# A gated recurrence with a gated feed-forward layer on one core: smaller feed-forward groups, split prefix sums, transposes by DMA, one pool of PSUM banks and a new order

## The chip, the cores and the metric

The kernel runs on one core of a Trainium2 chip. The time is the device time of one execution in microseconds (us); a kernel's figure is the median of its runs. Beside the times there is one profiled execution, whose span (first to last instruction) the views below are cut from. A core has five engines with a queue of instructions each, worked off in order: TensorE (PE, matrix products into PSUM), VectorE (DVE), ScalarE (ACT), GpSimd (POOL) and SyncE (SP, which issues most DMAs). PSUM has eight banks of 512 f32 columns in each of 128 partitions.

## The reference

Two stages. The first is a linear recurrence over 768 steps for 4 x 8 heads with a state of 48 x 48:

```python
mag = np.sqrt(a_re * a_re + a_im * a_im)
scale = np.minimum(mag, 0.999) / (mag + 1e-06)
a_re_n, a_im_n = (a_re * scale, a_im * scale)
for t in range(S):
    new_re = ar * S_re - ai * S_im
    new_im = ar * S_im + ai * S_re
    kv = np.einsum('bhd,bhe->bhde', k[:, :, t], v[:, :, t])
    S_re, S_im = (new_re + kv, new_im)
    y[:, :, t] = np.einsum('bhd,bhde->bhe', q[:, :, t], S_re)
```

The second takes y as 3072 tokens of 384 numbers: `gate = 1 / (1 + exp(-(x @ w_gate)))`, `val = x @ w_val`, result `(gate * val) @ w_out`, with 1536 inner columns (12 blocks of 128). Inputs and output are f32.

## The kernel before, in words

**Tiling.** The sequence is cut into 6 chunks of 128 steps. A slab is one chunk of one batch element, all 8 heads: 128 partitions (steps) x 384 columns (8 heads x 48). There are 24 slabs, chunk by chunk, in seven groups (`SIZES`: five of four slabs, two of two). The recurrence becomes, inside a chunk, a masked product of scores, and between chunks a state of 128 x 384 per batch element that is decayed and added to.

**Steps of a slab**, by the names that the order uses:

- `lr`, `la`: loads of a_re, a_im (L559, 192 KB each, in rows of 48 numbers). `sq`, `add`, `min` (L566 to L589): squares, sum, cap; `lna`, `lnm` logarithms; `inv` = exp(-ln a_re); `r` = a_im x inv; `atan` the angle (L687).
- `cl` (L618): the running sum of log magnitudes along the chunk, as an f32 product with a constant triangle `wl_t`; `ee` its exponentials; `scr`, `rbe`, `arr`: the last row goes through DRAM to become the decay of the state.
- `lk`, `lq`, `lv`: loads of k, q, v; `v16` casts v; `qke` multiplies q and k with `ee`.
- `ct` (L701 or L723): the running sum of the angle, in turns, as an f32 product with `wt_t`; `r16`, `nid` subtract the whole turns; `cr` keeps the last row for the next chunk, which `hop` adds into the next chunk's first row, one DMA for each slab (L714), or, in chunk 1, a product with `sel_t`. `ab`, `cs` (L766): absolute value, sine, cosine into an SBUF tile `cs`.
- `ks`, `qs` (L782): k and q times cosine and sine, as f16, 128 x 8 x 128. `tp` (L820): 16 transposes on PE and copies `qkT` (L827) for slabs 0 to 12; for slabs 13 to 23 (`CROSS`) two transposing DMAs on SP (`xk`, `xq`, L803).
- `sc` (L839), `mst` (L847): scores and mask; `kv`, `u`, `x16`, `P`: the state; `y` (L905, L907) and `y16`, its copy to f16; `xp`, `xt` (L925, L931): three transposes on PE and a copy give y with columns along partitions.

**Steps of a group's feed-forward part (MoE)**: for each of the 12 blocks `pg` and `pv` (L944), three products each over all slabs of the group at once (512 columns for four slabs, 256 for two); `tanh` on ACT (L954), `p` = (tanh + 1) x val on DVE (L960). For each slab `po` (L980), 12 products of 384 columns, `ot` (its eviction) and `st` (the store on SP). The weights come in nine casting DMAs on POOL's queue (`wg`, `wv`, `wo`).

**PSUM.** Two pools of four banks: `gen` for the recurrence, `moe` for the feed-forward part. One tile takes one bank.

**What sets the order.** Each step has a due time in the table `TIMES`. `Plan.order` sorts all steps by it, and the instructions go to their engines' queues in that sequence, so each queue, SP's and POOL's among them, is a fixed list. `SLOTS` says which buffer of its kind each tile takes. Where an engine changes its set of functions, a table load is put in (L1008). `WARM` puts filler products on `zero` ahead of some steps (L1014), 150 in all. `eng`, `scaled`, `SQV`, `ABV` and `ULATE` choose the engine of some elementwise steps.

Of the kernel before, what the change touches and what calls it, by code (L numbers as in the profile page):

```python
# [26 lines left out]
CROSS = 13  # L27
EASE = 0
ULATE = 4
BRISK = 1  # L30
PAIR = 2
PECARRY = 1
SQV = range(4, 9)
ABV = range(2, 9)
# [3 lines left out]
        22.939, 53.604, 46.761],  # L38
    "wv": [
        41.489, 57.377, 49.918],  # L40
    "wo": [
        69.384, 65.792, 74.71],
    "lr": [
        0.6, 2.76, 4.68, 1.01, 7.56, 11.4, 21.96, 9.48, 29.035, 36.763,
        34.603, 40.603, 53.574, 65.05, 65.46, 69.488, 91.541, 102.449, 94.661,
        101.489, 129.641, 144.257, 166.92, 169.283],
    "la": [
        1.42, 5.64, 6.6, 3.72, 8.52, 13.32, 21, 14.28, 30.955, 37.723, 44.224,
        38.683, 56.839, 59.355, 66.25, 71.918, 91.951, 100.699, 93.701,
        100.289, 132.576, 136.865, 169.693, 171.783],  # L50
    "sq": [
        5.29, 9.13, 10.09, 7.21, 12.09, 16.953, 26.869, 17.819, 35.119,
        43.141, 51.317, 50.58, 63.932, 71.041, 72.995, 77.727, 96.326, 108.9,
        100.923, 107.686, 141.821, 149.617, 173.785, 176.745],
    "add": [
        6.159, 9.999, 11.044, 8.079, 13.107, 17.97, 27.886, 19.639, 42.886,
        44.046, 52.222, 58.417, 64.837, 72.97, 75.53, 81.618, 99.728, 109.941,
        101.828, 108.978, 146.191, 151.929, 174.69, 177.65],
    "min": [
        10.579, 11.624, 21.17, 29.665, 54.424, 59.948, 80.715, 83.639,  # L60
        111.798, 110.895, 156.229, 185.814],
    "lna": [
        10.958, 34.211, 53.348, 80.235, 115.074, 157.704, 179.252],
    "lnm": [
        12.335, 32.834, 62.547, 84.606, 112.957, 159.31, 186.78],
    "inv": [
        13.712, 36.423, 64.669, 81.743, 117.191, 158.572, 180.12],
    "r": [
        16.087, 15.221, 39.728, 37.968, 67.623, 70.424, 89.8, 94.764, 118.736,
        126.526, 159.477, 181.025],  # L70
    "cl": [
        13.863, 16.67, 20.01, 15.378, 36.319, 37.411, 34.836, 38.883, 64.65,
        68.978, 65.942, 65.296, 86.871, 112.147, 102.388, 106.72, 115.007,
        117.823, 134.023, 131.882, 160.664, 162.183, 192.729, 188.19],
    "ee": [
        15.356, 20.801, 21.541, 20.061, 37.8, 38.54, 35.683, 39.73, 66.046,
        69.825, 68.557, 72.255, 87.718, 114.334, 111.477, 112.217, 116.451,
        118.669, 137.956, 136.74, 161.511, 163.03, 193.576, 189.037],
    "scr": [
        23.34, 22.65, 23.62, 22.37, 44.634, 48.008, 43.366, 48.288, 94.111,  # L80
        85.572, 83.333, 75.858, 96.031, 114.89, 112.033, 112.773, 118.11,
        120.772, 143.977, 139.687, 185.698, 186.798, 194.287, 194.567],
    "rbe": [
        31.915, 61.755, 97.571, 116.08, 149.099, 193.468, 197.428],
    "lk": [
        19.08, 12.36, 23.9, 10.44, 30.542, 22.93, 46.624, 26.99, 86.538,
        74.318, 80.523, 75.448, 103.409, 82.923, 106.289, 108.241, 133.536,
        118.468, 143.567, 127.135, 153.417, 186.388, 158.185, 173.993],
    "lq": [
        20.04, 18.12, 27.942, 16.2, 39.643, 35.803, 47.598, 49.079, 89.103,  # L90
        79.105, 83.883, 76.705, 104.369, 95.621, 107.249, 112.313, 135.905,
        125.596, 148.689, 134.624, 157.07, 193.058, 158.595, 187.724],
    "lv": [
        15.24, 17.16, 35.013, 42.956, 54.152, 67.21, 41.563, 81.87, 92.361,
        85.162, 115.54, 96.581, 105.329, 118.878, 87.987, 130.695, 139.277,
        121.052, 148.279, 126.005, 185.978, 192.648, 170.823, 177.453],
    "v16": [
        20.593, 42.309, 50.738, 49.342, 66.832, 77.757, 59.371, 87.463,
        98.286, 94.188, 124.976, 103.369, 118.084, 149.97, 105.026, 147.632,
        171.078, 133.794, 189.145, 130.048, 191.369, 202.109, 188.569, 183.572],  # L100
    "qke": [
        23.805, 22.502, 32.19, 20.947, 45, 47.581, 55.616, 60.85, 96.525,
        88.039, 91.561, 85.702, 112.701, 115.256, 128.287, 134.657, 148.209,
        164.194, 152.883, 143.564, 162.433, 196.377, 194.498, 198.138],
    "atan": [
        17.39, 41.764, 76.35, 105.833, 131.576, 183.842, 183.105],
    "ct": [
        18.918, 20.953, 26.326, 21.761, 43.292, 45.031, 52.079, 49.241,
        90.692, 86.225, 90.046, 89.232, 122.944, 118.469, 127.422, 128.468,
        141.143, 143.731, 163.053, 166.071, 196.201, 198.47, 197.014, 210.201],  # L110
    "r16": [
        19.765, 22.036, 28.601, 24.671, 44.785, 46.524, 55.711, 53.381,
        92.893, 87.268, 96.023, 92.427, 124.789, 119.316, 128.465, 129.397,
        145.892, 151.604, 163.899, 167.878, 197.481, 201.212, 205.333, 211.683],
    "nid": [
        21.599, 22.636, 29.201, 25.271, 47.8, 47.124, 57.969, 53.981, 95.223,
        89.07, 97.975, 98.138, 125.513, 120.184, 129.686, 131.483, 151.699,
        153.161, 165.483, 170.802, 198.308, 205.144, 206.601, 216.88],
    "cr": [
        25.889, 26.259, 30.065, 26.629, 49.053, 49.423, 59.91, 56.806, 95.586,  # L120
        95.956, 102.136, 104.169, 125.876, 126.246, 130.049, 132.953, 152.062,
        156.041, 176.375, 174.522],
    "cs": [
        23.575, 24.732, 30.542, 29.067, 49.793, 48.055, 58.646, 56.019,
        97.088, 89.752, 102.535, 99.273, 126.617, 120.704, 130.419, 133.335,
        153.726, 154.883, 165.847, 171.166, 198.671, 205.507, 207.141, 217.243],
    "ks": [
        25.137, 27.735, 34.253, 31.008, 53.847, 50.186, 62.767, 63.633,
        100.35, 91.041, 105.9, 103.014, 130.62, 121.993, 133.214, 138.058,
        155.016, 167.012, 173.321, 172.455, 201.678, 209.351, 208.486, 218.665],  # L130
    "qs": [
        26.003, 29.533, 35.985, 36.851, 56.177, 51.783, 69.053, 65.696,
        101.548, 97.554, 107.254, 108.12, 132.348, 123.325, 143.227, 141.296,
        157.143, 168.81, 175.386, 177.145, 203.143, 210.817, 215.684, 219.531],
    "ab": [
        30.542, 29.067, 49.12, 48.055, 58.364, 55.245, 97.088],
    "tp": [
        31.002, 27.003, 30.555, 36.965, 39.976, 38.436, 40.822, 42.338,
        64.204, 60.921, 63.757, 63.31, 71.142, 78.268, 80.861, 67.236,
        111.701, 114.56, 108.014, 104.329, 119.514, 113.24, 112.793, 121.647,  # L140
        155.897, 136.164],
    "qkT": [
        33.056, 33.654, 37.717, 38.315, 42.217, 39.084, 41.618, 43.881,
        65.097, 61.569, 67.856, 64.499, 73.684, 79.317, 83.445, 68.455,
        112.348, 115.942, 110.784, 109.586, 120.713, 114.145, 113.546,
        124.191, 156.545, 146.957],
    "sc": [
        39.752, 39.529, 41.273, 44.584, 47.577, 44.807, 46.784, 48.678,
        69.624, 75.674, 80.638, 79.114, 78.044, 81.308, 86.002, 84.728,
        117.176, 119.961, 115.653, 114.337, 127.199, 125.29, 117.599, 126.326,  # L150
        158.294, 153.974, 148.462, 148.686, 161.31, 159.167, 162.829, 160.041,
        177.84, 180.206, 182.371, 190.582, 191.856, 193.375, 188.836, 189.059,
        217.265, 217.042, 220.489, 220.712, 225.009, 222.435, 227.095, 226.217],
    "mst": [
        40.553, 39.953, 42.815, 45.85, 48.521, 45.251, 47.456, 49.586, 71.295,
        77.073, 81.062, 79.916, 78.711, 81.732, 86.669, 85.212, 117.6,
        121.312, 116.54, 115.343, 127.866, 126.187, 118.666, 126.786, 158.718,
        154.398, 148.887, 151.004, 161.781, 160.25, 163.254, 162.381, 179.769,
        180.968, 186.393, 191.006, 192.589, 193.799, 190.083, 189.483,
        218.066, 217.466, 220.913, 221.978, 227.064, 223.102, 227.663, 229.162],  # L160
    "kv": [
        40.622, 58.131, 77.844, 72.884, 102.188, 82.829, 122.094, 117.399,
        132.528, 134.669, 150.851, 145.025, 166.717, 170.965, 176.345,
        179.358, 201.706, 211.495, 207.411, 220.935],
    "P": [
        41.152, 60.655, 78.245, 74.282, 104.834, 84.746, 122.859, 118.2,
        142.162, 135.07, 153.269, 145.426, 169.676, 178.704, 183.373, 181.567,
        204.867, 213.384, 212.918, 221.512],
    "y": [
# [131 lines left out]
}  # L301
WARM = {
    ('cl', 0): 41,
    ('cl', 2): 8,
    ('cl', 3): 2,
    ('ct', 0): 7,
    ('ct', 2): 16,
# [737 lines left out]
```

## Time and profile before

| | us |
|---|---|
| median of 3 runs | 265.34 (264.82 to 265.72) |
| profiled execution, span | 263.2 |
| PE busy | 240.2 |
| DVE busy | 211.7 |
| ACT busy | 178.5 |
| POOL busy | 150.7 |
| DMA moved | 38.12 MB, mean 145 GB/s |

The page cuts the span into 40 equal slices of 6.6 us and gives each engine's busy share in tenths, the TensorE clock granted (PEclk) and the share of the 16 DMA engines. A group's line gives the source line, engine, operation, result and operands with shapes, the count, the busy sum and the mean time in ns of one, and then the engine's idle time ahead of it with what ended it. Products overlap in the pipeline, so their busy times are longer than the distance from one start to the next; the chain gives starts. The costliest groups by line:

| line | step | engine | count | mean ns |
|---|---|---|---|---|
| L944 | pg, pv of 512 columns | PE | 360 | 379 |
| L980 | po | PE | 276 | 326 |
| L960 | p of 512 | DVE | 60 | 682 |
| L954 | tanh of 512 | ACT | 60 | 606 |
| L847 | mst | DVE | 48 | 685 |
| L680 | qke | POOL | 20 | 1915 |
| L618 | cl, f32 | PE | 48 records | 557 |
| L931 | xt copy | DVE | 24 | 352 |
| L507 | y16 / ot | DVE | 24 / 23 | 551 |

### The profile page before, as it was taken

How to read it: one execution, taken by the hardware profiler on the slowest of the kernel's cores; microseconds unless marked ns; L12 is line 12 of the kernel's file. 1: busy time of each engine (PE TensorE's matmuls, PEld its weight loads, DVE VectorE, ACT ScalarE, POOL GpSimd, SP SyncE). 2: the span in 40 equal slices, each digit the busy share in tenths (PEclk: the TensorE clock that was granted, in tenths of full speed). 3: DMA queues.
4: the chain of work that ended last, by engine and by line, in shares of the span. 5: the costliest groups of instructions: out<-in, count | busy, mean ns of one | idle time of the engine just before them, and what ended most of it. 6: DMA issues, size and time to landing. Idle time of an engine off the chain costs nothing.

```text
span 263.2 us, 5644 instructions
## 1 busy us (share of the span) xinstructions
PE 240.2 (91%) x2066; PEld 150.2 (57%) x2066; DVE 211.7 (80%) x363; ACT 178.5 (68%) x288; POOL 150.7 (57%) x165
## 2 busy tenths in 40 slices
PE   6076598999999999999999999999999999999995
PEld 6043375454657654547765456654457544679784
DVE  2658998798988979979997889898859689987453
ACT  3799698299999478999469648758974373214240
POOL 3035409969599999679877299833687642010000
PEclk9669989999999999999999999999999999999999
DMA  7999999999999939975699969859964455651011
GB/s 146 218 214 176 192 149 188 205 166 182 139 205 202 181 74 169 176 157 95 121 209 204 151 135 149 194 111 178 221 133 90 66 110 108 73 147 36 8 54 60
DMA packets 174859, 38.12 MB, mean 145 GB/s; under 512 B 167768, under 2 KB 174832, under 8 KB 174832
## 3 DMA queue, kind: packets, MB, share of 16 engines
q1 hardware_dynamic: 170336, 34.20, 68.3%
q0 software_dynamic: 4496, 3.57, 9.7%
q8 instruction: 16, 0.26, 0.4%
q14 instruction: 11, 0.09, 0.1%
HBM read 30.74 MB, written 4.76 MB: 135 GB/s over the span
## 4 chain that ended last, share of the span: by engine, by line
PE 58%; ACT 15%; DMA 8%; DVE 7%; SPq 4%; issue 3%; POOL 3%; ACTq 0%; POOLq 0%
PE o L980 16%; PE v L944 13%; PE g L944 11%; PE cl L618 4%; ACT L1008 4%; DMA a<-in_a_im_dram 3%; PE sc L839 3%; SPq L541 3%; PE ct L723 3%; DMA a<-in_a_re_dram 3%; ACT a L687 2%; POOL qk L680 2%; DMA qk<-in_q_dram 2%; ACT g L954 1%; POOL a L609 1%
## 5 line engine op out<-in xcount | busy, mean ns | idle before, releaser
L954 ACT ACTIVATE g<-g 128x512 f16<-128x512 f32 (+1 forms) x84 | 43.6, 542 | 37.4 <-PE g L944 34.5
L960 DVE SCALAR_TENSOR_TENSOR p<-g,v 128x512 f16<-128x512 f16 (+1 forms) x84 | 49.6, 607 | 20.9 <-ACT g L954 10.1
L944 PE MATMUL v<-xt,wv 128*128 128x512 f16 (+1 forms) x252 | 57.3, 348 | 0.5 <-ACT g L954 0.4
L944 PE MATMUL g<-xt,wg 128*128 128x512 f16 (+1 forms) x252 | 56.9, 348 | 0.5 <-DVE xt L931 0.3
L980 PE MATMUL o<-wo,p 128*128 128x384 f16 (+1 forms) x300 | 54.6, 319 | 0.5 <-ACT g L954 0.5
L577 POOL TENSOR_TENSOR lm<-sq 128x384 f32<-128x384 f32 x20 | 23.2, 1174 | 30.7 <-DVE sq L568 18.9
L680 POOL TENSOR_TENSOR qk<-qk,ee 128x768 f32<-128x768 f32 x20 | 38.2, 1915 | 2.4 <-ACT ee L627 1.6
L847 DVE TENSOR_TENSOR mst<-sc,msk_t 128x512 f16<-128x512 f32 x48 | 32.3, 685 | 4.7 <-PE sc L839 4.6
L944 PEld LDWEIGHTS <-wv 128*128 128x128 f16 x252 | 24.1, 98 | 20.6 <-issue 1.6
L980 PEld LDWEIGHTS <-p 128*128 128x128 f16 x300 | 27.3, 97 | 14.9 <-issue 0.9
L944 PEld LDWEIGHTS <-wg 128*128 128x128 f16 x252 | 23.6, 97 | 20.3 <-issue 2.6
L618 PE MATMUL cl<-lm,wl_t 128*128 128x384 f32 x48 | 22.2, 557 | 9.2 <-ACT lm L598 8.9
L1008 ACT ACT_TABLE_LOAD x23 | 29.5, 1283 | 0.4
L782 DVE TENSOR_TENSOR qst<-qk,cs 128x768 f16<-128x768 f32 x24 | 26.1, 1092 | 0.0
L782 DVE TENSOR_TENSOR kst<-qk,cs 128x768 f16<-128x768 f32 x24 | 24.4, 1029 | 1.4 <-ACT cs L772 0.9
L609 POOL TENSOR_TENSOR a<-a 128x768 f32<-128x768 f32 x10 | 18.1, 1816 | 9.1 <-DMA qk<-in_q_dram 7.8
L571 ACT ACTIVATE sq<-a 128x768 f32<-128x768 f32 x19 | 16.0, 846 | 6.3 <-DMA a<-in_a_im_dram 6.2
L861 POOL TENSOR_TENSOR state<-state,arr 128x384 f32<-128x384 f32 x16 | 13.9, 869 | 11.0 <-DVE state L889 10.7
L827 DVE COPY qkT<-tp 128x1024 f16<-128x1024 f16 x26 | 17.3, 682 | 1.5 <-PE tp L821 1.5
L625 ACT ACTIVATE ee<-cl 128x384 f32<-128x384 f32 x24 | 12.0, 500 | 9.0 <-PE cl L618 6.9
L839 PEld LDWEIGHTS <-qkT 128*128 128x128 f16 x192 | 13.4, 97 | 7.4 <-issue 2.7
L723 PE MATMUL ct<-a,wt_t 128*128 128x384 f32 x40 | 16.9, 507 | 0.6 <-ACT a L687 0.5
(76 smaller groups left out, 428.9 us busy)
## 6 DMA issues: line engine op xcount, KB each, us to landing
a<-in_a_re_dram SPq DMA_DIRECT2D x24, 192.0 KB
a<-in_a_im_dram SPq DMA_DIRECT2D x24, 192.0 KB
qk<-in_k_dram SPq DMA_DIRECT2D x24, 192.0 KB
v<-in_v_dram SPq DMA_DIRECT2D x24, 192.0 KB
qk<-in_q_dram SPq DMA_DIRECT2D x24, 192.0 KB
out_dram<-ot SPq DMA_DIRECT2D x23, 192.0 KB
wg<-in_moe_w_gate_dram POOLq DMA_DIRECT2D x3, 384.0 KB, 6.4
wv<-in_moe_w_val_dram POOLq DMA_DIRECT2D x3, 384.0 KB, 6.4
```

Source lines behind the costliest of these rows:

```text
L577: eng(g).tensor_tensor(out=T[LM][:, s], in0=T[SQ][:, 0], in1=T[SQ][:, 1], op=ALU.add)
L618: nc.tensor.matmul(T[CL][:, :HD], wl_t, T[LM][:, s], start=True, stop=True)
L680: eng(g).tensor_tensor(out=T[QK], in0=T[QK], in1=T[EE], op=ALU.mult)
L723: nc.tensor.matmul(T[CT][:, :HD], wt_t, T[A][:, 1, s], start=True, stop=False, skip_group_check=True)
L782: nc.vector.tensor_tensor(out=T[SL][i].rearrange("p h (r x) -> p h r x", r=2)[:, :, :, 0:D], in0=heads(T[QK][:, i]).unsqueeze(2) .broadcas ...
L839: nc.tensor.matmul(sc[:, i], kt, qt, start=True, stop=True)
L847: nc.vector.tensor_tensor(out=T[MS], in0=T[SC], in1=msk_t.unsqueeze(1).broadcast_to([L, 4, L]), op=ALU.mult)
L944: nc.tensor.matmul(T[ACC][:, :nt], w[:, j, fb * 128:fb * 128 + 128], T[XT][:, j, :nt], start=(j == 0), stop=(j == 2))
L954: nc.scalar.activation(out=T[G16][:, :nt], in_=T[PG][:, :nt], func=FT.Tanh, scale=0.5)
L960: nc.vector.scalar_tensor_tensor(out=T[PT][:, fb, :nt], in0=T[G16][:, :nt], scalar=1.0, op0=ALU.add, in1=T[PV][:, :nt], op1=ALU.mult)
L980: nc.tensor.matmul(T[PO][:, :wd], T[PT][:, fb, s * L:(s + 1) * L], wo16[:, fb, c0:c0 + wd], start=(fb == 0), stop=(fb == NFB - 1))
L1008: nc.scalar.preload_act_table_set(SETS[key[1]])
```

## The change

Seven things at once:

- **MoE groups of two slabs.** `pg`, `pv`, `tanh`, `p` run over pairs of slabs (256 columns), two blocks of 128 inner columns in one bank, so that `tanh` and `p` still take 512 elements. 12 pairs x 6 double blocks.
- **Prefix sums as two f16 passes** for groups 2 to 6 (`SPLIT`, slabs 8 to 23): the operand is split into a high and a low f16 part (`lh`, `ll` for the logarithms, `th`, `tl` for the angles), and `cl` and `ct` are two f16 products each. The cap is taken after the logarithm there.
- **Cosine and sine in PSUM.** `ct`'s result lies in the second of two neighbouring banks, `ab` writes the first, both sines are taken in place, and `ks`, `qs` read them from PSUM.
- **y by transposing DMA** on SP (`xt`, slabs 4 to 23, `YCROSSED`), with no `xp` and no copy. q and k go by DMA from slab 9 on (`CROSSED`) instead of 13.
- **The hop by group.** The last rows of a chunk go to DRAM (`car`, on SP) and come back in one adding DMA per group.
- **One pool of eight PSUM banks** (`bank`), with views cut from one tile.
- **A new order**: new `TIMES`, `SLOTS` and `WARM` (26 fillers), and a table `HOME` that names the engine of each elementwise step; table loads go from 23 to 31.

Counts of instructions: DVE 48 `mst`, 72 `p`, 18 `qkT`, 14 `y16`, 12 `ot`, 8 `v16`, 7 `sq`, 10 `ab`, 8 `ll`, 8 `tl`; ACT 17 `sq`, 10 `y16`, 11 whole `ot` and 2 halves, 5 `v16`, 14 absolute values, 72 `tanh`; POOL 23 `qke`, 11 `v16`, 11 `x16`, 5 hops, 8 `r`, 7 `lh`, 5 `th`; SP 30 transposes of q and k and 20 of y. The core of the diff:

```diff
-CROSS = 13
+CROSSED = range(9, 24)
+YCROSSED = range(4, 24)
+SPLIT = range(2, 7)
+HOME = {
+    "sq": "aaavvvvaavaaaaaaavvaaaaa",
+    "y16": "aavvvavaavvvaaaavavvvvvv",
+    "ot": "vvavvvvaavvaaavvaavvaaaaa",
...
-    t_gen = kind("gen", 4, [L, 512], F32, psum)
-    t_moe = kind("moe", 4, [L, 512], F32, psum)
+    banks = psum.tile([L, 8, 512], F32, name="banks")
...
+            def e2(T, LM=LM, LH=LH, i=i, j=j, w=w):
+                home("lh", w).tensor_scalar(
+                    out=T[LH][:, 0, i:j], in0=T[LM][:, i:j], scalar1=LNCAP,
+                    scalar2=1.0, op0=ALU.min, op1=ALU.mult)
...
+                nc.vector.scalar_tensor_tensor(
+                    out=T[LH][:, 1, i:j], in0=T[LM][:, i:j], scalar=LNCAP,
+                    op0=ALU.min, in1=T[LH][:, 0, i:j], op1=ALU.subtract)
...
-                nc.tensor.matmul(T[CL][:, :HD], wl_t, T[LM][:, s],
-                                 start=True, stop=True)
+                for i in range(2):
+                    nc.tensor.matmul(T[CL][:, :HD], wl16, T[LH][:, i, s],
+                                     start=not i, stop=bool(i))
...
+                    nc.tensor.matmul(
+                        T[CS][:, 1, :HD], wt16 if split else wt_t,
+                        turns(T)[:, s, i] if split else T[A][:, 1, s],
+                        start=not i, stop=False, skip_group_check=True)
...
-                nc.scalar.activation(out=cs[:, 1], in_=ct, func=FT.Sin,
-                                     scale=TWO_PI)
+                nc.scalar.activation(out=T[CS][:, 1, :HD], in_=T[CS][:, 1, :HD],
+                                     func=FT.Sin, scale=TWO_PI)
...
-                    nc.gpsimd.dma_start(
-                        T[A][:1, 1, s], T[CRP][32 * b + 31:32 * b + 32],
-                        accum_op=ALU.add)
+                    nc.sync.dma_start(car[c - 1], T[CRP][31::32])
+                nc.gpsimd.dma_start(
+                    T[A][:1, 1, :n], car[c - 1][lo:lo + n].unsqueeze(0),
+                    accum_op=ALU.add)
...
+            if m in YCROSSED:
+                def e(T, Y16=Y16, XT=XT, s=s):
+                    nc.sync.dma_start_transpose(out=T[XT][:, s % PAIR],
+                                                in_=T[Y16])
...
-                    for j in range(3):
-                        nc.tensor.matmul(
-                            T[ACC][:, :nt], w[:, j, fb * 128:fb * 128 + 128],
-                            T[XT][:, j, :nt], start=(j == 0), stop=(j == 2))
+                        for r in range(2):
+                            f0 = (2 * fp + r) * 128
+                            for j in range(3):
+                                nc.tensor.matmul(
+                                    T[ACC][:, r], wt[:, j, f0:f0 + 128],
+                                    T[XT][:, :, j], start=(j == 0),
+                                    stop=(j == 2))
```

## The prediction

> **What bounds the kernel now.** I read four views: the page's slices, the busy times by stretch, the chain that ended last with its single pieces, and the groups by shape.
>
> ```profile
> PE 240.2 (91%) x2066; PEld 150.2 (57%) x2066; DVE 211.7 (80%) x363; ACT 178.5 (68%) x288; POOL 150.7 (57%) x165
> PE   6076598999999999999999999999999999999995
> PEclk9669989999999999999999999999999999999999
> DMA  7999999999999939975699969859964455651011
> ```
>
> The span has two parts. A ramp, in which PE has little to do while DMA is at 9 tenths, and a long stretch in which PE is full. The first real gate product stands at 58.65 us in the chain. The stretches (span, then PE, weight load, DVE, ACT, POOL, clock, DMA share, GB/s):
>
> ```profile
> 0.00:58.60 58.60, 40.58 (x345) 26.94 (x346) 44.12 (x81) 43.35 (x60) 27.89 (x37) 0.88 1.02 184
> 58.60:87.00 28.40, 28.35 (x239) 16.85 (x239) 25.12 (x37) 28.00 (x40) 24.53 (x29) 1.00 1.13 183
> 87.00:115.00 28.00, 26.99 (x199) 14.82 (x198) 25.41 (x39) 21.89 (x37) 23.85 (x23) 1.00 0.85 160
> 191.00:235.00 44.00, 43.97 (x371) 26.06 (x371) 35.88 (x63) 18.99 (x35) 19.93 (x24) 1.00 0.55 105
> ```
>
> From 58.6 to the last product at 260 PE is busy 199.6 of 201.3 us. The worst long stretch (87 to 115) has 96.4%. So the kernel is ramp 58.65 + PE work 201.3 + a tail of 3.3 (last eviction and store) = 263.2. DVE is second, at 88% even while PE is full. What PE's work costs there is read from consecutive starts in the chain, since busy records overlap:
>
> ```profile
> 205.28 0.17 PE xp L925 x3
> 206.15 0.65 PE g L944 x3
> 206.80 0.16 PE ct L737
> 206.96 0.65 PE ct L723 x2
> 233.51 0.22 PE sc L839 x4
> 235.27 0.33 PE v L944 x3
> ```
>
> An f32 product of 384 columns (L723, recorded as x2) takes 0.65, an f16 one of the same width (L737) 0.16. Three gate products 512 wide take 0.65, three 256 wide 0.33: the same per column.
>
> **The change, part by part. PE.** (1) Prefix sums of slabs 8 to 23 as two f16 passes: 16 cl and 16 ct go from 0.65 to 2 x 0.16, 32 x 0.33 = 10.6 us less. Both prices are rows of this trace, so the bounds are close (cl also shows 0.70: 11.4). (2) y by DMA for slabs 4 to 23: 60 PE transposes at 0.17/3 = 0.057, 3.4 less. (3) q and k by DMA from slab 9 on instead of 13: 64 transposes, 3.6 less. (4) MoE groups of two slabs: 864 products 256 wide against 360 of 512 and 144 of 256; by the rows above the time is the same (94 us), and tanh (L954) and gate product (L960) keep their 512-element shape with two blocks per bank. Sum: 17.6 us of PE. In the full stretch each of them is on the path, since nothing but PE bounds there.
>
> **The ramp.** The first gate product needs slabs 0 and 1 instead of 0 to 3. By the due times of the two orders, 36 input loads of 192 KB and 4 weight loads of 384 KB (as landed) stand ahead of it, against 47 and 5. That is 8.65 MB against 11.2; at the 184 GB/s of the first stretch, 47 us. The other gate is DVE: 75 instructions instead of 83 are queued ahead of its first gate product; at starts 0.47 apart for 384 elements, 0.6 for 512 and 1024, 0.87 for 768, that is 39 us instead of 45, and at today's density (45 in 60) 52 us for the first p, 50.5 for the product before it. I take 49; the bounds are 45 (58.65 scaled by bytes) and 55 (as now, less only the wait from the first pair's transposed y to the second's, 55.1 to 58.6, the DVE copies at 54.78 and 57.98). Ahead of the product PE then does 18.2 us of real work instead of 21.1 (3 sel/ct statements and a nid fewer, partly against kv), so 2.9 us move behind it. The order issues 26 filler products instead of 150, 6 of them ahead of the MoE. The clock in slices 2 and 3 is 0.6, and there a cl took 1.66 instead of 0.65. If it fell back so, the chain's own PE pieces of one slab (cl 0.65, ct 0.65, nid 0.16, transposes 0.46, scores 0.22, y 0.2) would double: 0 to +2.3, inside the bounds.
>
> [...]
>
> **Other engines** (today's means). DVE gains 16 low parts (ll, tl) of 768 elements at 0.95 as L568 = +15.2, 8 v16 at 0.3 to 0.56, say 0.4 = +3.2, two sq and two r at 0.95 = +3.8, three ab +1.7, lh/th +1.7, u and x16 +0.9; it loses 21 xt at 0.352 = 7.4, 10 y16 at 0.55 = 5.5, 11 whole and 2 half ot = 6.8, 8 qkT at 0.68 = 5.4, 3 qke = 3.2, and 1.9 in p. Net -3.7: 208 us. ACT gains 8 table loads:
>
> ```profile
> L1008 ACT ACT_TABLE_LOAD x23 | 29.5, 1283 | 0.4
> L782 DVE TENSOR_TENSOR qst<-qk,cs 128x768 f16<-128x768 f32 x24 | 26.1, 1092 | 0.0
> L803 SPq DMA_TRANSPOSE qkT<-qst x11: 1231/1286/2125, 130.5 to 229.4; - x11
> SPq L803 <- DVE p L960: 11.7, 4, 4.9
> ```
>
> that is +10.3, and 22 evictions at 0.49, two half ones, 9 copies at 0.52 and a th, less two sq and three abs: +24 in all, 202 us. POOL loses 15 (13 v16, 11 hops, 5 x16, 2 r, against 3 qke and 5 th). These ride under PE while they keep up. Behind the ramp, whose share I scale by the queued work (DVE 44.1 x 39/45 = 38, ACT 43.4 x 58/66 instructions = 38), DVE stands at (208-38)/187 = 91% and ACT at (202-38)/187 = 88%, against 83% and 67%. The stretch at 58.6 shows both that high (88% and 99%) with PE full, so it can be done, with less slack. I let PE fall from 99.2% to 97.5%, between today and the 96.4% of 87 to 115: 4.8 us given back; bounds 0 and 7 if today's rows carry over, up to 13 by the rival below.
>
> Cosine and sine in PSUM removes no instruction. Two of eight banks are held from ct to qs (some 6 us a slab, against one bank and about 4.5): about 24 x 7.5 = 180 bank-us more out of 1,500 (8 banks, 187 us). It is covered by the freer pool; without the cover PE waits, which is inside the give-back. The kst/qst group shows a mean of 1.03 and 1.09 with a median of 0.95: 24 x (0.08 + 0.14) = 5.2 us of stretching, single ones to 2.02 while POOL runs. I count 0, with 0 to 5.2 less as bounds. [...]
>
> SP: 28 transposes and 4 car stores more. At 1.28 each SP is held 36 us longer (an xt moves 3 blocks, not 8, so 0.5 to 1.28), and the 22 of before waited 35 us in all, 1.6 each. Queued behind each are the loads, with sq, qke and v16 waiting for them, and the scr and out stores. The transposed y is late by its issue and transfer, perhaps 3 us against 0.6 for transposes and copy; the gate products wait for it, covered by other groups' output products (0.65 a piece). The car store adds a trip ahead of hop (3.1 us to landing), under the MoE of the group before; uncovered, five times 3.
>
> **Sum.** 49 + (201.3 - 17.6 + 2.9 = 186.6, at 97.5% instead of 99.2%: +4.8 = 191.4) + 3.3 = 243.7, that is 19.5 below the profiled 263.2. The profiled execution stands 2.1 below the median of 265.34, so 246.
>
> **Rivals.** (a) PE is no longer the bound: DVE, with ACT beside it, sets the pace. For: 91% asked where the stretches from 87 to 235 show 86% (127 of 148). 170 us at 86% are 198 us: 49 + 198 + 3.3 = 250, plus 2.1 = 252; where the last 28 us can't be filled (55% now), 9 more: 252 to 261. The DMA rings give nearly the same: 38.1 + 4.1 MB (8 transposes of 262 KB, 20 of 98) with 1.2 in the last 28 us is 41 MB at 184 GB/s = 223 + 28 = 251; against it, slices of 259 GB/s. (b) Slower: the SP queue, in order, makes the loads late. Its issues now sum to 205 us of the 231 in which it is used, stretched to 2 to 5 us a piece wherever the rings are full (at the least durations, 0.37 for a load and 1.23 for a transpose, they would be 89). 28 x (1.28 + 1.6) = 81 more; if only the free 26 takes it up, loads slip by 55 at the end; half of that reaching PE gives 246 + 27 = 273. It decides once 20 us of slip reach PE. For: up to 88 us SP is never free. Against: behind 117 us it has gaps of several us, 12 of the 15 q/k pairs and 12 of the 20 xt are due later than that, and the 35 us of waits of now cost PE nothing visible. (c) The change doesn't do what it says: no gain from f16 passes would give back 10.6 and make 257. The L737 row makes this unlikely.
>
> **Numbers.** The forecast 0.58, spanning 237 to 252; (a) with (c) 0.24; (b) 0.15; no change 0.03. The range 236 to 258 holds the first nearly whole and most of (a): 236 is the 45 us ramp with nothing given back and cl at its 0.70, 258 the 55 us ramp with about 11 given back. Runs of this kernel tell 0.3% (0.8 us) from no change: faster 0.82, same 0.03, slower 0.15.
>
> **What would show it.** The first gate product near 49 us, PE above 97% from there, cl and ct as two f16 passes in 0.32 in the chain, DVE near 208 and ACT near 202, SP's waits on transposes (35 now) under 60. The forecast is wrong if PE idles more than 10 us behind the ramp, or the ramp passes 55: then the reading of which engine holds PE, not the count of PE's work, has failed.

## The result, and the profile after

The changed kernel takes 317.52 us (median of 4 runs, 316.14 to 324.62) where the kernel before takes 265.08 us (median of 4, 264.54 to 265.72): a ratio of 1.1971, 95% interval 1.1932 to 1.2009. The run of 324.62 us had a lower granted clock, 0.894 against 0.908, and is not in the ratio. The forecast was 246. The profiled execution spans 314.4 us.

The page of the changed kernel, its busy times and the slices of TensorE and its clock:

```profile
PE 237.2 (75%) x2178; PEld 175.5 (56%) x2178; DVE 207.1 (66%) x334; ACT 200.6 (64%) x313; POOL 147.8 (47%) x140
...
PE   0094899995997937598968649779759699779396
...
PEclk9998799999599996979999959887969789979989
```

The first line was forecast well: DVE 207.1 (208 expected), ACT 200.6 (202). But the row of nines that PE had in the kernel before is gone, and the granted clock dips with it. The stretch from the first gate product to the end, for the kernel before and then for the changed one (span, PE, weight load, DVE, ACT, POOL, clock, DMA share, GB/s):

```profile
58.60:263.20 204.60, 199.60 (x1721) 123.30 (x1720) 167.62 (x283) 135.19 (x229) 122.78 (x129) 1.00 0.72 134
```

```profile
48.60:314.40 265.80, 210.34 (x1985) 158.31 (x1982) 170.37 (x263) 162.44 (x261) 122.23 (x108) 0.90 0.68 126
```

The first gate product starts at 48.6 us, where 49 was forecast. All that went wrong lies behind it: 265.8 us instead of 194.7 (191.4 and the tail of 3.3). PE is busy 210.3 of them instead of 186.6, and idle 55.5 instead of 8.1. Those two, 23.7 and 47.4, less the 0.4 of the ramp, are the whole error of 70.7 in the span. The busy part is nearly all clock: the granted clock behind the ramp is 0.90, and with the same number of products, 2178, the kernel x11 below has PE busy for 214.1 us at 0.986 over the whole run, against 237.2 at 0.908 here.

Who waits for whom, over the whole span (engine, tile and line, what ended the wait: us, times, longest):

```profile
POOL qk L732 <- DMA qk<-in_q_dram: 23.8, 8, 5.6
...
PE banks L1054 <- DMA xt<-y: 19.8, 8, 4.8
...
PEld L922 <- DMA qkT<-kst: 12.2, 4, 5.7
...
ACT sq L592 <- DMA a<-in_a_im_dram: 10.7, 5, 3.4
```

Four kinds of transfers are late at once: the loads of q and k, the transposed y (`xt`), the transposed k, the loads of a. In the kernel before no DMA stands among the waits ahead of PE, whose largest are:

```profile
PE cl L618 <- ACT lm L598: 8.9, 2, 8.8
PE ct L737 <- DVE r L730: 3.8, 3, 1.9
```

What these four share is SyncE's queue, and these are its own waits at the y transposes (L1016):

```profile
SPq L1016 <- DVE y L523: 19.0, 3, 8.0
...
SPq L1016 <- DVE banks L839: 13.8, 2, 7.5
...
SPq L1016 <- DVE state L979: 10.5, 2, 7.0
```

All waits at L1016 add up to 69.9 us, those at the q and k transposes (L881) to 26.9: 96.8 for transposes, against 35 before. One such stand in the timeline of SyncE (start, duration, what is issued):

```profile
116.45 1.27 SPq L881 DMA_TRANSPOSE qkT<-kst  x1
117.77 0.57 SPq L561 DMA_DIRECT2D v<-in_v_dram  x1
126.11 1.19 SPq L1016 DMA_TRANSPOSE xt<-y  x1
127.34 0.57 SPq L561 DMA_DIRECT2D a<-in_a_re_dram  x1
127.96 0.53 SPq L747 DMA_DIRECT2D car<-cr  x1
128.54 0.45 SPq L561 DMA_DIRECT2D a<-in_a_im_dram  x1
129.09 2.01 SPq L881 DMA_TRANSPOSE qkT<-kst  x1
```

For 7.8 us, from 118.3 to 126.1, SyncE issues nothing, because y of one slab isn't ready (ScalarE's copy of it ends at 126.1). Then come, in one burst, the two loads, the carry and the k transpose that stood behind it. In the window from 110 to 130 us PE is busy 12.8 of 20 us at a clock of 0.83.

### The profile page after: what moved, and what is told of

It is laid out like the page before. It is cut to its first block, busy times and chain, and to the rows that moved or that the text cites. A ratio compares the mean times of both kernels' runs of the same rounds, so it can differ in the third digit from the quotient of the medians.

```text
span 314.4 us, 5826 instructions
## 1 busy us (share of the span) xinstructions
PE 237.2 (75%) x2178; PEld 175.5 (56%) x2178; DVE 207.1 (66%) x334; ACT 200.6 (64%) x313; POOL 147.8 (47%) x140
## 2 busy tenths in 40 slices
DMA packets 191309, 42.24 MB, mean 134 GB/s; under 512 B 184200, under 2 KB 191280, under 8 KB 191280
## 4 chain that ended last, share of the span: by engine, by line
PE 26%; DMA 12%; SPq 6%; DVE 4%; issue 3%; POOL 3%; ACT 3%; DVEq 0%; POOLq 0%; ACTq 0%
PE banks L1054 15%; PE banks L1093 6%; DMA xt<-y 4%; DMA rbe<-scr 3%; DMA qkT<-kst 2%; SPq L561 2%; SPq L1016 2%; PE banks L922 2%; SPq L881 1%; DMA out_dram<-ot 1%; DMA a<-in_a_im_dram 1%; DVE p L1072 1%; DVE mst L937 1%; DVE y L523 1%; POOL state L951 1%
## 5 line engine op out<-in xcount | busy, mean ns | idle before, releaser
L1054 PE MATMUL banks<-xt,wg 128*128 128x256 f16 x432 | 63.3, 295 | 20.0 <-DMA xt<-y 15.9
L1065 ACT ACTIVATE g<-banks 128x512 f16<-128x512 f32 x72 | 42.0, 596 | 45.1 <-PE banks L1054 35.7
L1054 PE MATMUL banks<-xt,wv 128*128 128x256 f16 x432 | 64.6, 295 | 4.6 <-DMA xt<-y 3.9
L1054 PEld LDWEIGHTS <-wg 128*128 128x128 f16 x432 | 44.3, 105 | 33.1 <-issue 19.1
L732 POOL TENSOR_TENSOR qk<-qk,ee 128x768 f32<-128x768 f32 x23 | 43.6, 1896 | 40.2 <-DMA qk<-in_q_dram 23.8
L1072 DVE SCALAR_TENSOR_TENSOR p<-g,banks 128x512 f16<-128x512 f16 x72 | 48.0, 681 | 17.9 <-ACT g L1065 12.4
L1093 PE MATMUL banks<-wo,p 128*128 128x384 f16 (+1 forms) x300 | 56.2, 327 | 0.0
L1054 PEld LDWEIGHTS <-wv 128*128 128x128 f16 x432 | 44.7, 106 | 19.6 <-issue 7.4
L937 DVE TENSOR_TENSOR mst<-banks,msk_t 128x512 f16<-128x512 f32 x48 | 32.2, 684 | 22.9 <-PE banks L922 21.4
L860 DVE TENSOR_TENSOR kst<-qk,banks 128x768 f16<-128x768 f32 x24 | 22.7, 947 | 8.6 <-POOL qk L732 7.8
L600 POOL TENSOR_TENSOR lm<-sq 128x384 f32<-128x384 f32 x20 | 20.7, 1039 | 16.4 <-ACT sq L592 10.1
L922 PEld LDWEIGHTS <-qkT 128*128 128x128 f16 x192 | 15.1, 108 | 23.7 <-DMA qkT<-kst 12.2
L860 DVE TENSOR_TENSOR qst<-qk,banks 128x768 f16<-128x768 f32 x24 | 22.7, 945 | 0.0
L631 POOL TENSOR_SCALAR lh<-lm 128x768 f16<-128x768 f32 x7 | 19.4, 2780 | 3.7 <-ACT lm L613 3.5
L667 PE MATMUL banks<-lm,wl_t 128*128 128x384 f32 x16 | 7.9, 612 | 15.6 <-ACT lm L613 15.6
```

What stands on the lines that cost most here:

```text
L600: home("add", m).tensor_tensor(out=T[LM][:, s], in0=T[SQ][:, 0], in1=T[SQ][:, 1], op=ALU.add)
L631: home("lh", w).tensor_scalar(out=T[LH][:, 0, i:j], in0=T[LM][:, i:j], scalar1=LNCAP, scalar2=1.0, op0=ALU.min, op1=ALU.mult)
L732: home("qke", m).tensor_tensor(out=T[QK], in0=T[QK], in1=T[EE], op=ALU.mult)
L860: nc.vector.tensor_tensor(out=T[SL][i].rearrange("p h (r x) -> p h r x", r=2)[:, :, :, 0:D], in0=heads(T[QK][:, i]).unsqueeze(2) .broadcas ...
L922: nc.tensor.matmul(sc[:, 4 * hf * both + i], kt, qt, start=True, stop=True)
L937: nc.vector.tensor_tensor(out=T[MS][:, :n_], in0=T[SC], in1=msk_t.unsqueeze(1).broadcast_to([L, n_, L]), op=ALU.mult)
```

## The experiments

All are single runs, with the kernel before at 264.5 to 265.2 us on the same chip each time. Since the first gate product comes anywhere from 46.6 to 48.9 us in runs whose ramp is not touched, I compare the rest: the span from the first gate product to the end. It is 204.6 in the kernel before, 265.8 in the changed one, 194.7 in the forecast.

| run | time | first gate product | behind it | PE busy behind it |
|---|---|---|---|---|
| changed kernel (profiled execution) | 314.4 (span) | 48.6 | 265.8 | 210.3 |
| x1_y_const | 269.76 | 48.5 | 219.5 | 194.6 |
| x2_moe_free | 311.19 | 46.9 | 262.6 | 207.3 |
| x3_y_by_pe | 266.42 | 46.7 | 218.0 | 197.5 |
| x5_y_by_pe_lh_dve | 267.57 | 48.5 | 217.3 | 196.2 |
| x9_no_y_transposes | 264.17 | 48.9 | 213.5 | 195.0 |
| x10_no_y_qk_const | 258.47 | 48.6 | 208.2 | 190.5 |
| x11_no_y_qk_lh_dve | 252.66 | 46.6 | 204.4 | 188.0 |
| x12_no_y_qk_st_const | 256.46 | 47.0 | 207.5 | 190.7 |
| x16_no_y_sc_const | 257.16 | 46.7 | 208.7 | 191.7 |
| x17_qk_const | 310.89 | 47.1 | 262.0 | 206.6 |
| x18_no_qk_loads | 299.66 | 48.6 | 249.3 | 201.4 |

**SyncE's stand at y, and with it the products' dependence on y.**

```diff
 nc.sync.dma_start_transpose(out=T[XT][:, s % PAIR],
-                            in_=T[Y16])
+                            in_=ycon)
```

> The changed kernel; the transposing DMAs of y (slabs 4 to 23) read a constant tile in place of y16, so y is left out of the result's path: SP no longer waits at them for y16, and the gate products no longer hang on y; as many DMAs of the same size run. Theory A (SP stands in order at the y transposes, so the loads behind come late): 317 falls to 265 or less, POOL's waits for q loads (23.8 us) all but vanish. Rival B (only the trip of y through DMA holds PE, 28 us of PE's waits): about 290. Rival C (the order itself, whatever is in it): over 300.

269.76 us. The same 20 transposes are issued and carried, and the same 42.24 MB move, but SyncE no longer waits for y16 and nothing of the feed-forward part hangs on y: 46.3 us less behind the ramp, 30.6 of PE's idle time and 15.7 of its busy time. TensorE's row and its clock in this run:

```profile
PE   0076589999959979898999697974999999999795
PEclk9999689999998997999999999998699999999999
```

So neither the transposes' share of the DMA engines nor the rest of the new order makes the 46 us.

**The products' wait for xt, alone.**

```diff
-                                    T[XT][:, :, j], start=(j == 0),
+                                    xcon[:, :, j], start=(j == 0),
```

> The changed kernel; the gate and value products read a constant tile in place of xt, so y is left out of the result's path there, but SP still waits for y16 at each y transpose. Theory A: SP's waits stay and with them the late loads: over 290. Rival B (the trip of y holds PE): 290 or less, PE's waits on xt (28 us) gone. Rival C: over 300.

311.19 us, 3.2 less behind the ramp. The 19.8 us that PE had waited for xt are gone, and the lateness comes out at the next transfer instead:

```profile
PE banks L924 <- DMA qkT<-kst: 19.3, 4, 7.7
PE banks L669 <- ACT lm L615: 15.4, 1, 15.4
```

(The second line is the wait of the ramp, 15.6 us in the changed kernel.)

**y on TensorE again, all else of the change kept.**

```diff
-YCROSSED = range(4, 24)
+YCROSSED = ()
```

The steps `xp` and `xt` get a due time and a free bank in gaps of the plan.

> The changed kernel with one part undone: y of slabs 4 to 23 is transposed by three products on PE and a copy on DVE or ACT, at due times between y16 and the first gate product, in banks that the plan leaves free; 3.4 us of PE and 7 us of DVE more, 20 DMAs fewer. Theory A and rival B both: 317 falls to 280 or less. Rival C (the order, not the way of y): within 10 us of 317.

266.42 us, 47.8 less behind the ramp, though the products depend on y as before and PE has 60 transposes more. So, with x2, it is SyncE's stand that costs, not the products' dependence on y.

**y by DMA in the kernel before.**

```diff
+YCROSSED = range(4, 24)
...
+                if m in YCROSSED:
+                    nc.sync.dma_start_transpose(
+                        out=T[XT][:, :, s * L:(s + 1) * L], in_=T[Y16])
+                    return
```

(with four buffers of y16)

> The kernel before with one part added: y of slabs 4 to 23 by transposing DMA on SP, at the place where the copy of xt stood; PE has 3.4 us less, DVE 7 us less. Theory A: 265 rises to 285 or more, since SP stands at each of the 20. Rival B: 265 rises by PE's waits for the trip, 5 groups of some 3 us: 275 to 285. Rival C (the new order is to blame): within 6 us of 265.

289.83 us, 25 more than the kernel before. The part does harm by itself, and half as much as in the new order. Here it shows at the products themselves, which wait 21.1 us for xt, while SyncE's waits at the y transposes are 15.7 us; x4 does not tell the one from the other.

```profile
PE g L953 <- DMA xt<-y: 13.8, 4, 5.6
PE v L953 <- DMA xt<-y: 7.3, 1, 7.3
```

**What carries the lateness from SyncE to PE.** In x17 SyncE does not wait for k and q at their transposes, x18 leaves out the loads of q and k; both keep the y transposes and SyncE's waits at them (69.9 and 82.6 us).

```diff
 nc.sync.dma_start_transpose(
-    out=T[D_], in_=T[SL][i].rearrange("p h x -> p (h x)"))
+    out=T[D_], in_=qcon)
```

> The changed kernel with its y transposes and their waits as they are, and only the DMA transposes of q and k reading a constant tile (the scores of slabs 9 to 23 are left out). SyncE still stands some 70 us at the y transposes. Theory A1: what comes late behind these stands is chiefly the loads: 300 to 315. Theory A2: chiefly the q and k transposes, that is qkT for the score products: 275 to 295.

310.89 us, in the range of theory A1; 3.8 less behind the ramp. But these transposes still stand in the queue behind those of y, and PE still waits 11.6 us for them. What their lateness alone costs this run does not show.

```diff
-                    dma_in(T[QK][:, i], src, b, c)
...
-                home("qke", m).tensor_tensor(out=T[QK], in0=T[QK], in1=T[EE],
-                                             op=ALU.mult)
+                home("qke", m).tensor_tensor(
+                    out=T[QK], in0=lcon.unsqueeze(2).broadcast_to([L, 2, HD]),
+                    in1=T[EE], op=ALU.mult)
```

> The changed kernel with its y transposes and their waits as they are, and without the loads of q and k (left out; the scaled q and k are made of a constant). Theory A1 (late loads): GpSimd's 24 us of waits for q go, and the time falls to 275 to 295. Theory A2 (late q and k transposes): 300 to 315. If both x17 and this stay above 300, what is late is y's own trip in a chain through SyncE's order, which neither takes away.

299.66 us, between the ranges of the two theories; 16.5 less behind the ramp, where A1 asked for 22 and more. The loads of q and k are thus the largest single carrier found, and not all of the 16.5 need be their lateness, since their 9.4 MB are gone too. Some 30 of the 46 us are left to the others: here GpSimd waits 21.0 us for the decays that go through DRAM and ScalarE 15.8 for loads of a, all from the same queue.

```profile
POOL arr L705 <- DMA rbe<-scr: 21.0, 4, 14.6
...
PE banks L1057 <- DMA xt<-y: 16.9, 8, 4.7
ACT sq L594 <- DMA a<-in_a_im_dram: 15.8, 6, 3.6
```

How the 30 divide among these I did not measure.

**Without any work for y.** x9 leaves the transposes out altogether, which is what the sum of the prediction had taken the edit for.

```diff
-                    nc.sync.dma_start_transpose(out=T[XT][:, s % PAIR],
-                                                in_=T[Y16])
+                    pass
```

and the products read `xcon`, as in x2.

> The changed kernel without the transposes of y of slabs 4 to 23 at all (left out; all gate and value products read a constant tile instead of xt), so that neither TensorE nor SyncE nor the DMA engines have any work for them. This is what the prediction's sum took the edit for. If the trips of y are the one step that failed and the rest of the sum holds, 241 to 252. If something else in the change costs as well (the missing 17 us of x3_y_by_pe, 266.4), 256 to 266, and the waits ahead of TensorE name it.

264.17 us, in the second of the two ranges: y was not the one step that failed. Against x1 it is 6.0 us less behind the ramp: that is about what the 20 transposes cost when SyncE need not wait at them. Its row behind the ramp:

```profile
48.90:262.40 213.50, 195.00 (x1985) 151.48 (x1982) 175.64 (x263) 160.59 (x261) 123.93 (x108) 0.97 0.80 148
```

PE idles 18.5 us there, and its work still runs at a clock of 0.97. From here the parts were taken off one by one.

**q and k.** x10 is x9 with the edit of x17; x16 is x9 with the products, not SyncE, reading the constant.

> As x9_no_y_transposes, and the DMA transposes of q and k of slabs 9 to 23 read a constant tile, so that SyncE waits for none of them (the transposes are still issued and carried; the scores of these slabs are left out). If SyncE's stands at the q and k transposes, with loads queued behind, hold what is left, 8 to 15 us less than x9; if they are harmless, as the kernel before suggests with 35 us of such waits, within 3 us of x9.

> x9_no_y_transposes (264.2) with the DMA transposes of q and k as they are, SyncE waiting for kst and qst, but all products of slabs 9 to 23 that read the transposed q and k read a constant tile instead: TensorE waits for none of these trips. x10 took 5.7 us off x9 by freeing SyncE and TensorE both. If those 5.7 us are SyncE's stands with loads behind them, this stays at 262 to 265; if TensorE's own wait for the trips, it falls to 257 to 260 as x10.

258.47 and 257.16 us, 5.3 and 4.8 less behind the ramp. x16 has it nearly all, while SyncE still stands 34.4 us at these transposes (36.3 in x9). So the 5 us do not come from SyncE's stand; what x10 and x16 share is that PE need not wait for these trips. My reading in x10's expectation was wrong. PE's waits for the trips in x9 add up to only 2.5 us, though, and most of the gain is PE's busy time (195.0, then 190.5 and 191.7), that is, clock (0.97, then 0.99 and 0.98). How much of it is the trips' own is not shown.

**Stores.** x12 is x10 with the stores taken from a constant.

> x10_no_y_qk_const with every store of the output taken from a constant tile (the result itself isn't stored), so that SyncE waits for no ot either (32 us of its waits in x10), though it issues the same stores. Theory A carried on: SyncE's queue in order, now at the stores, still makes the loads of q and k late (one of them, 5.0 us, is on x10's chain of waits): 4 to 8 us less than x10. If loads have slack by then: within 2 us of 258.5.

256.46 us, of which 1.6 came in the ramp; 0.7 behind it. SyncE's waits for `ot`, 32 us in x10, cost next to nothing here.

**lh on VectorE.**

```diff
-    "lh": "vgvgggggggvg",
+    "lh": "vgvgvvvvvvvv",
```

> x10_no_y_qk_const with the seven lh on VectorE. Behind the ramp TensorE still idles some 17.7 us in x10 (256.8 of span, less 48 of ramp, less 191.1 busy), and lh on GpSimd is on its chain of waits at 146.8 and 153.8 us, and ahead of three of TensorE's waits (cl, 3.7 us). Theory L: with SyncE's stands gone, lh shows its price, 4 to 8 us less than x10 (250 to 254). Rival: GpSimd has slack between, or VectorE takes back what GpSimd gives: within 2 us of 258.5, as x5 showed against x3.

> As x3_y_by_pe (the y transposes of slabs 4 to 23 back on TensorE, 266.4 us), and the seven rounded minima lh that GpSimd made (2.78 us each, 19.4 in all) on VectorE instead. Theory L: what x3 still lacks against the sum of the prediction (17 us: 266.4 against some 249) lies largely in lh, which stands ahead of the prefix sums and, on GpSimd, ahead of the states u; two of them were on the chain of waits between 70 and 130 us, with TensorE idle for 11 of those 60 us. Then 252 to 259, GpSimd's busy time down by 19, VectorE's up by 4 to 8. Rival: VectorE at 18 to 19 of 20 us is what holds x3, and more work on it makes 264 to 272. If it is neither, 262 to 266.

x11 (on x10) takes 252.66 us: 3.8 less behind the ramp, 2.0 more by a shorter ramp. x5 (on x3) takes 267.57, only 0.7 less behind the ramp, in the range of its rival. The seven minima cost 4 us where nothing else is late, 2.5 of them in PE's busy time, and next to nothing otherwise. x11, which leaves out what y, q and k have to wait for, is the fastest run of the study, and its row is the one to hold against the kernel before:

```profile
46.60:251.00 204.40, 188.04 (x1985) 148.60 (x1982) 173.95 (x270) 160.04 (x261) 102.98 (x101) 1.00 0.86 154
```

PE's work is 188.0 at full clock, as the sum had it (186.6). But 204.4 us behind the ramp is what the kernel before needs too (204.6), though its PE is busy for 11.6 us more of them. x11 is faster by its ramp alone.

**Other orders.** Six runs compute everything in another order, and all missed.

```diff
+AHEAD = 12.0
...
-    t_qk = kind("qk", 5, [L, 2, HD], F32)
-    t_v32 = kind("v32", 3, [L, HD], F32)
+    t_qk = kind("qk", 7, [L, 2, HD], F32)
+    t_v32 = kind("v32", 4, [L, HD], F32)
```

The loads are due up to 12 us earlier, as far as a buffer is free.

> The changed kernel with all its DMA transposes, but the loads of q, k, v and a asked for up to 12 us earlier in SyncE's order, as far as two more buffers for q and k and one more for v allow. Theory A says that SyncE stands at the transposes of y and all that is queued behind comes late; if the loads are what matters of that, 280 to 298; if it is rather the transposes of q and k and the trips of y themselves that come late, 308 to 318.

> x5_y_by_pe_lh_dve with its loads asked for earlier as in x6_loads_ahead. If SyncE's remaining stands (105 us of waits in x3, the transposes of q and k with loads behind them) still reach TensorE, 4 to 8 us less than x5; if loads no longer bind, within 1.5 us of x5.

327.62 and 305.36 us: 10 more than the changed kernel, 38 more than x5, outside all the ranges. The loads were due just as their buffers came free, and SyncE now stood at loads with the transposes behind: 27.5 us in x6 (4.7 in the changed kernel), 40.9 in x8 (12.1 in x5). From x8's view of SyncE's waits (L640 is the loads):

```profile
SPq L640 <- PE banks L871: 23.7, 4, 8.7
```

PE waited 15.8 us in that run for a transposed q (three times, up to 8.2). It looks like the same mechanism with another instruction at the head of the queue; no run took it apart.

```diff
-YCROSSED = range(4, 24)
+YCROSSED = range(4, 20)
+TRIP, COVER = 5.0, 9.0
...
+        order = self.listed(at)
```

The transposes are due 5 us later, the MoE steps of their slabs 9 us. `listed` gives out all buffers and banks anew; a step whose buffer is taken goes later.

> The changed kernel, y by DMA for slabs 4 to 19 (20 to 23 on TensorE), but the order is made anew: the transposes of y are due 5 us later and the MoE steps of those slabs 9 us later against everything else, with 5 buffers for y16 and 4 for xt. Theory A (SyncE is asked to wait for y too early, and the products too early for the trip): SyncE's wait at the y transposes falls from 69.9 us to under 25, the granted clock is back over 0.96, and the time is 258 to 278. Rival: the price is that of the transposes themselves (some 1.2 us of issuing each, their landing and their share of the DMA engines), which no order takes away: over 300.

310.63 us, in the range of the rival. SyncE's wait at y fell to 23.7 as expected, and xt is not among PE's large waits, but neither brought the time down:

```profile
ACT g L1127 <- PE banks L1116: 51.9, 22, 11.0
...
PE banks L1057 <- POOL x L592: 8.8, 1, 8.8
PE banks L1116 <- ACT g L1127: 8.6, 8, 2.5
```

The moved steps now wait for one another, with PE in front of ScalarE's tanh and ScalarE behind PE's products. The rival's reason, the price of the transposes themselves, does not explain it: x1 carries all 20 and takes 269.76. Whether a trip with full cover would be free stays open.

> A kernel that computes everything: the changed kernel, y of slabs 4 to 23 transposed on TensorE and lh on VectorE as in x5_y_by_pe_lh_dve (267.6), and slack for SyncE: stores up to 6 us later in its order with 4 buffers of ot, 6 of qk, 4 of v32; banks and steps without a place take the first free one. If SyncE's stands at stores and at loads (some 40 us of waits in x5) reach TensorE, 259 to 264; if only those at the q and k transposes do, 265 to 269.

> As x13_y_pe_lh_dve_slack, with q and k of slabs 9 to 12 on TensorE too (by DMA from slab 13 on, as in the kernel before): some 3.6 us more of TensorE's work, eight transposes fewer on SyncE. If SyncE's stands are what x10 took away, 1 to 5 us less than x13; if x10 gained by TensorE's own waits on the trips, or not at all, 2 to 5 us more.

> As x13_y_pe_lh_dve_slack, with no DMA transpose left: q and k of all slabs on TensorE (15 slabs more, some 13.6 us of TensorE's work, and 30 copies on VectorE). By theory A SyncE runs free and TensorE is full: 48.6 of ramp, 186.6 + 3.4 + 13.6 of work at 97.5 %, 3.3 of tail and 2.1 around it: 263. Over 268 if VectorE (some 230 of 260 us) sets the pace instead.

281.26, 286.51 and 299.27 us (edits: later stores and more buffers; with it `CROSSED = range(13, 24)`; with it `CROSSED = range(24, 24)`). All three are listed anew as in x7, with every buffer given out by what is free, and all three lose behind the ramp to x5 (229.0, 235.9 and 249.3 against 217.3). PE idles ahead of its products' weight loads (20.3 us in x13, 13.8 in x5) with nothing that the profile shows as the reason. Since the new places come on top of the edits, the three do not tell what SyncE's stands cost in x5; x15, with no transposing DMA left, is the slowest of them. Not run was y's transpose on another engine's queue. No version that computes everything beat the kernel before.

## Why the prediction was wrong

**The ramp: right.** 48.6 us against 49. Two slabs instead of four stand ahead of the first product, and the loads and VectorE's queue were counted well.

**PE's work: right as a count.** 188.0 at full clock in x11, against 186.6. The f16 passes do what they say: the two products of a `ct` or `cl` take 0.33 us together where one f32 product took 0.65. Rival (c) is out. One `ct` of two f16 passes in the chain of x10:

```profile
135.15 0.33 PE banks L796 x2
```

**The step that failed first: SP.** The prediction counted 28 transposes on SyncE and wrote that "the 35 us of waits of now cost PE nothing visible", that the transposed y is late by "perhaps 3 us" and that this is "covered by other groups' output products". The sum so carried the edit at nothing. x1 and x3 put SyncE's stand at 46 to 48 us behind the ramp, x2 the products' own wait for xt at 3, and x1 against x9 the 20 transposes themselves at 6. Of the 71.1 us that the stretch behind the ramp took too long, 52.3 go with y (x9). The mechanism stood there as rival (b), at 0.15, and the case came out 44 us above its 273. Two sizes in it were too small. It took the wait of the old q and k transposes, 1.6 us each. But y16 is the last step of a slab's recurrence, and SyncE reaches its transpose in the list before it is done: 69.9 / 20 = 3.5 us each, and up to 8.2; at all transposes SyncE waits 61 us more than in the kernel before, where rival (b) added 45. And it let 27 us of the slip reach PE, where 46 to 48 did. The issues that it has "stretched to 2 to 5 us a piece wherever the rings are full" are mostly shorter: the kernel before has 205 of them, which sum to 164 us; ten take 2 us or more, the longest 3.89, and a load's (L541) has a median of 0.45 us in slices of 2 us with a DMA share under 0.5 and of 0.76 in those with 1 or more. In the view of before no wait ahead of PE is put down to a DMA; the new waits stand with loads, carries and other transposes due behind them. The part costs 25 us in the old order (x4) and 46 to 48 in the new. Two reasons can be argued for the difference, and neither was run: late loads make the next y later, and so SyncE's next stand longer; and in the new order's table the first products are due 0.1 to 2.4 us after xt in nine of the ten pairs.

**The clock: not in the sum.** Of the 70.7 us, 23.7 are PE's busy time, and all but the 1.4 that x11 has too are work gone slow. The prediction weighed a slower clock in the ramp alone, at 0 to 2.3 us. In the changed kernel the trace's record of the clock has ten stretches at half clock behind the ramp, 51.2 us together; the kernel before has half clock from 8.1 to 18.3 us and from 32.0 to 35.4, and none behind its ramp. Gate products of 256 columns (L1054) start 0.109 us apart at full clock and 0.213 at half clock (medians). PE is busy for 42.0 of the 51.2 us, and half of that, 21.0, is nearly the whole loss. So in the changed kernel a stall of PE was paid for half as much again: 23.7 beside 47.4.

The sum of the idle time does not decide: in x15 the idle times ahead of the gate products and their weight loads (L1119) add up to 34.7 us at a clock of 0.977 over the run, in x9 (L1055) to 9.9 at 0.961. In the changed kernel's record the clock changes at the edges of equal steps of 3.41 us. Behind the ramp 48 steps at full clock had less than 1.70 us of PE's idle time, and none of them was followed by half clock; of five with 1.70 to 1.96 us one was, and all nine with 2.09 to 2.79. Of the 15 steps at half clock the ten with less than 0.4 us of idle time led back to full clock, the five with 0.67 to 3.26 did not. In the kernel before no step behind the ramp has more than 0.65 us. These are counts of two traces; what sets the clock they do not show. The zeros of the constant tiles are not what lifts it: x2 has them and 0.906 over the run, x3 works on y and has 0.974.

**The give-back: too small by half.** With y gone altogether (x9) PE idles 18.5 us behind the ramp, where 8.1 were allowed (4.8 given back and the tail), and its work takes 195.0 instead of 186.6. From x9 over x16 and x10 to x11 the work falls to 191.7, 190.5 and 188.0, as the clock behind the ramp rises from 0.97 to 0.98, 0.99 and 1.00; the idle time falls only to 17.0, 17.7 and 16.4. So of the 9.1 us that lie between x9 and x11, 7.0 are PE's busy time, nearly all of it clock. lh was priced at 0.9 us on GpSimd from the old minimum L584, and takes 2.78:

```profile
L631 POOL TENSOR_SCALAR lh<-lm 128x768 f16<-128x768 f32 x7 | 19.4, 2780 | 3.7 <-ACT lm L613 3.5
```

Those 13.2 us (7 x 1.88) are more than all that GpSimd has over its forecast (147.8 against 136). What remains in x11, 9.7 us above the forecast's stretch and 16.4 idle, is near rival (a): 170 us of VectorE at 86% made its 252, and x11 has VectorE at 174 of 204.4 us (85%) and 252.66. That the two numbers agree shows no cause; no run took work off VectorE alone, so the cause of these 9.7 us stays open.

**Cosine and sine in PSUM: the gain at the edge of its bounds.** `kst` and `qst` now take 947 and 945 ns, after 1029 and 1092: 24 x (0.082 + 0.147) = 5.5 us of VectorE less, where 0 was taken and 5.2 was the bound. In the kernel before, the 23 of the 48 that ran with no GpSimd instruction beside them took 946 to 959 ns, and each of the eleven over 1 us (1084 to 2019) had one beside it; in the changed kernel 26 had GpSimd at work for over 90% of their time and took 933 to 954. Less load on VectorE is not the reason: x11, with VectorE busy for 210.5 of 251.0 us against 211.7 of 263.2 before, has 948 and 947. VectorE's total does not show the gain (207.1 us, 208 forecast), and no run shows what it was worth in time.

## What to carry to other kernels

Price a DMA that waits for computed data not by its issue and transfer but by how long its queue stands there (here 3.5 us each at y, for 1.20 of issue), and list what is queued behind it; here a transpose of the last result of a chain, put into the queue that also brings the inputs, made the next inputs late (GpSimd waited 23.8 us for loads of q and k). The waits that the queue has now are no evidence for the next ones (35 us before, 96.8 after): ask how early the list reaches the instruction, not how long it takes. To see it, take away the queue's wait (a constant source, which frees the consumer too) and then the consumer's wait alone: here 46 us against 3.

## What the runs showed of the hardware

- For 128x768 on GpSimd, a `min` with a multiplication by one from f32 to f16 took 2780 ns (`lh`, L631 of the changed kernel), the two-bound `min`/`max` f32 to f32 915 ns (L584 before), two multiplications f32 to f16 832 ns (`th`, L523 of the changed kernel). The first of these took 549 ns on VectorE in the changed kernel (one instruction) and 584 in x5 and x11 (eight each).
- In the changed kernel a y transpose of 128x384 held SyncE for 1.18 to 1.39 us in issue alone (median 1.20), nearly as long as one of q or k with 128x1024 (median 1.28 and 1.29): the issue did not follow the size.
- In the changed kernel the granted clock changed at the edges of steps of 3.41 us; behind the ramp each of the nine steps at full clock with 2.09 to 2.79 us of PE idle time was followed by one at half clock, none of the 48 with less than 1.70. In x15 34.7 us of idle time ahead of the gate products and their weight loads went with a clock of 0.977 over the run.
- The low part `ll`, with two SBUF inputs, took 952 ns (x11), 1072 (changed kernel) and 1477 (x5) at the same shape; what lay beside it was not tested.
